# Third group's attention visits two units later, and one key decay issued ahead of a value load

## The chip, the cores and the metric

The kernel runs on one core of one Trainium2 chip. The metric is the device time of one execution in microseconds. Before the change it was 212.03 us, the median of three runs (211.67, 212.03, 212.72).

## The reference

A decayed linear attention over 4 batches, 8 heads, 768 positions and head size 64, followed by a two-layer feed-forward block on the result, all taken by the kernel as float32 and rounded to float16 when loaded:

```python
for b in range(nb):                      # blocks of 64 positions
    intra = (qb @ kb.T) * Dmask          # Dmask[i, j] = lam ** (i - j) for i >= j, else 0
    intra = intra @ vb
    inter = (qb * lam_pow) @ kv_state
    out[block] = intra + inter
    kv_state = lam_block * kv_state + (kb * rev_pow).T @ vb
x = out as [3072 tokens, 512]
h = x @ w_in                             # 512 x 2048
g = h * tanh(softplus(h))                # Mish
result = g @ w_out                       # 2048 x 512
```

## The kernel before

The kernel works in chunks of 128 positions instead of 64. There are six chunk rows (groups n = 0 to 5) of four batches each, so 24 chunks, numbered c = 4n + b. Chunk 8 is the first of the third group, n = 2. All names below carry such a number in words only; in the profile the buffers of one name are not told apart.

For each chunk the loads bring k, q and v from memory (tiles `kn`, `qn`, `vz`; lines L68, L76, L79), all issued by POOL. The key is multiplied by its decay (`ktil`, line L266, function `scale_k`), on POOL for chunks 4 to 19. From the third group on, `turn` (L275) has SP issue two transposing transfers for each chunk, one for q (`qraw`, waits for the load of q) and one for the decayed key (`kraw`, waits for `ktil`).

The attention of a group of four chunks is done in **visits**, two chunks at a time: `pair_s` (L343, L349) multiplies `kraw` by `qraw` into `pS` and adds the state's part to `pO`; DVE masks `pS` into `sb` (L358); `pair_o` (L370) multiplies `sb` by `vz`; DVE scales the outcome into `xtok` (L376); and SP issues two transposing transfers `xt<-xtok` (L380). The four blocks of `xt` of one group are the input of the first feed-forward product of that group. `pair_a` (L319) brings the state forward: DVE adds (`raws`, L323) and POOL multiplies (`wc`, L324).

The feed-forward block is the dense work of PE. `mm1_unit` (L399, four matmuls with 512 columns) makes one of 16 slices of h for the whole group; ACT applies Mish to it (`hsg`, L406). `mm2_unit` (L431, four matmuls with 512 columns) makes a quarter of the output of one chunk; after the fourth quarter ACT copies `po` to `osb` (L446) and issues the store.

The order is written out by hand, and every engine keeps it. There are three stretches:

- **The head.** Groups 0 and 1 are done with PE transposes (`first_t`, L217: `pk` and `pq`), `first_s` (L237) and `first_o` (L252, L256); PE also runs the first group's `mm1_unit`s and then the second group's in pieces (`mm1_tile`, L417). POOL issues the loads of chunks 4 to 7 and the weights `wout` (L107) in a list, and between them the key decays of chunks 4 to 7.
- **The double period** (n = 1 of the last loop). PE runs 32 `mm2_unit`s, u = 0 to 31, for the first two groups. Into them the visits of the third group are set at the numbers in `steps`. POOL issues k and q of chunks 12 to 15 after units 7, 11, 15 and 19, v of chunks 12 and 13 after unit 23, and v of 14 and 15 after unit 27, each time behind a one-element copy (`tick`, L387) from the output tile that ACT has just written. `turn` of chunk 12 stands after unit 21 and that of chunk 13 after unit 23.
- **The single periods** (n = 2 to 5): 16 `mm1_unit`s and 16 `mm2_unit`s of one group, with the visits of the next.

Within one unit number, the visit is written ahead of the loads and of `turn`, since it is entered in `todo` first.

Of the kernel before, what the change touches and what calls it, by code (L numbers as in the profile page):

```python
# [13 lines left out]
def bc(ap, axis, n):  # L14
    shape = list(ap.shape)
    shape.insert(axis, n)
    return ap.unsqueeze(axis).broadcast_to(shape)
# [3 lines left out]
def kernel(  # L21
# [11 lines left out]
    B, H, S, D = q.shape  # L33
# [10 lines left out]
    NT = 2  # L44
# [13 lines left out]
    def chunk_rows(t, i):  # L58
        n, b = divmod(i, B)
        return t[b, :, n * C : (n + 1) * C, :].rearrange("h p c -> p h c")  # L60
# [9 lines left out]
    def load_q(i):  # L70
        if i == 0:
            qn[i] = const.tile([128, H, D], F32, name="qn0")
            nc.scalar.dma_start(out=qn[i], in_=chunk_rows(q, i))
            return
        qn[i] = loads.tile([128, H, D], F16, name="qn", tag="qn")
        nc.gpsimd.dma_start(out=qn[i], in_=chunk_rows(q, i))  # L76

    def load_v(i):
        nc.gpsimd.dma_start(out=vz[i % NVB][:, :, 0:D], in_=chunk_rows(v, i))  # L79
# [25 lines left out]
    def load_wout(s):  # L105
        w = DF // WS
        nc.gpsimd.dma_start(  # L107
            out=wout[s],
            in_=moe_w_out[s * w : (s + 1) * w, :].rearrange("(k p) f -> p k f", p=128),
        )  # L110
# [152 lines left out]
    def scale_k(i):  # L263

        t = work.tile([128, H, D], F16, name="ktil", tag="ktil", bufs=8)
        (nc.vector if i < B or i >= (NG - 1) * B else nc.gpsimd).tensor_tensor(  # L266
            out=t, in0=kn[i], in1=bc(lk, 2, D), op=ALU.mult)
        ktil[i] = t
# [117 lines left out]
    def behind(src):  # L386
        nc.gpsimd.tensor_copy(tick, src)  # L387
# [118 lines left out]
    for i in range(B, NVB - 2):  # L506
# [5 lines left out]
    load_k(NVB - 1)  # L512
    scale_k(B + 1)
    load_q(NVB - 1)
    load_v(NVB - 1)
    scale_k(B + 2)
    load_wout(0)
    load_wout(1)
    scale_k(B + 3)
# [4 lines left out]
    steps = {11: ((first_t, 4),), 13: ((first_s, 4),), 14: ((first_t, 5),),  # L524
             15: ((first_o, 4), (first_s, 5), (first_t, 6))}
# [14 lines left out]
    for f, i in ((load_k, c + 1), (load_q, c + 1), (load_k, c + 2), (load_q, c + 2)):  # L540
        f(i)
    steps = {(4, 0): ((first_o, 5), (first_s, 6)), (4, 1): ((first_t, 7), (state_step, 0)),
             (4, 2): ((first_o, 6), (first_s, 7), (state_step, 1)), (4, 3): ((state_step, 2),),
             (5, 0): ((first_o, 7), (state_step, 3))}
# [10 lines left out]
    for n in range(NT - 1, NG):  # L555
        dense = [(mm2_unit, m, b, part) for m in ((0, 1) if n < NT else (n,))
                 for b in range(B) for part in range(WS)]
        if n >= NT:
            dense = [(mm1_unit, n, ni) for ni in range(NKI)] + dense
        todo = {}  # L560

        def at(u, f, *args):
            todo.setdefault(u, []).append((f, args))

        if n + 1 < NG:
            pairs = []
            for b in (0, 2):
                s = Pair()
                s.n, s.b = n + 1, b
                pairs.append(s)  # L570
            steps = (((9, pair_s, 0), (13, pair_o, 0), (16, pair_s, 1), (20, pair_o, 1),
                      (24, pair_a, 1)) if n < NT else
                     ((4, pair_s, 0), (8, pair_o, 0), (13, pair_s, 1), (17, pair_o, 1),
                      (20, pair_a, 1)))
            for u, f, b in steps:
                at(u, f, pairs[b])
        if n == NT:
            at(0, lambda: behind(hsg[n][0:1, 0, 0:1]))
            at(0, turn, (n + 1) * B + 2)
            at(0, turn, (n + 1) * B + 3)  # L580
        if n + 2 < NG:
            c = (n + 2) * B
            loads_ = [(f, c + b) for b in range(B) for f in (load_k, load_q)]
            loads_ += [(load_v, c + b) for b in range(B)]
            for x, (f, i) in enumerate(loads_):
                if n >= NT:
                    u = (1, 2, 3, 5, 6, 8, 10, 11, 12, 13, 14, 15)[x]
                    at(u, lambda u=u: behind(hsg[n][0:1, u, 0:1]))
                else:
                    u = 7 + x // 2 * 4  # L590
                    if x % 2 == 0:
                        at(u, lambda: behind(last_out[0][0:1, 0:1]))
                at(u, f, i)
            for b, u in enumerate((21, 23) if n < NT else (18, 19, 21, 23)):
                at(u, turn, c + b)
        for u, (fn, *args) in enumerate(dense):
            fn(*args)
            for f2, args in todo.get(u, ()):
                if args and isinstance(args[0], Pair):
                    args[0].spare = "po" if u < NKI - 1 and n >= NT else "ph"  # L600
                f2(*args)
# [30 lines left out]
```

## Time and profile before

| what | value |
| --- | --- |
| time, median of three runs | 212.03 us |
| the profiled execution's own time | 213.28 us |
| its span, first to last instruction | 211.5 us |
| granted TensorE clock, mean | 1.000 |
| PE busy | 203.1 us, 96% of the span |
| POOL, ACT, DVE busy | 102.4, 86.3, 69.3 us |
| double period on PE | 54.9 to 87.4 us |
| transfers moved | 26.76 MB, mean 127 GB/s |

The span leaves 1.78 us of the execution's own time outside. A row of a timeline gives the start and the length in microseconds, then engine, line, operation, what is written and read, the count, and in brackets how long the engine had been idle and what released it. In a list of transfers, the last number is the time from the issue to the landing. A lone `PEld` is the weight load that runs beside PE's matmuls, and an engine's name with a `q` is its sequencer.

### The profile page before, as it was taken

How to read it: one execution, taken by the hardware profiler on the slowest of the kernel's cores; microseconds unless marked ns; L12 is line 12 of the kernel's file. 1: busy time of each engine (PE TensorE's matmuls, PEld its weight loads, DVE VectorE, ACT ScalarE, POOL GpSimd, SP SyncE). 2: the span in 40 equal slices, each digit the busy share in tenths (PEclk: the TensorE clock that was granted, in tenths of full speed). 3: DMA queues.
4: the chain of work that ended last, by engine and by line, in shares of the span. 5: the costliest groups of instructions: out<-in, count | busy, mean ns of one | idle time of the engine just before them, and what ended most of it. 6: DMA issues, size and time to landing. Idle time of an engine off the chain costs nothing.

```text
span 211.5 us, 4241 instructions
## 1 busy us (share of the span) xinstructions
PE 203.1 (96%) x1728; PEld 110.2 (52%) x1728; DVE 69.3 (33%) x131; ACT 86.3 (41%) x146; POOL 102.4 (48%) x149
## 2 busy tenths in 40 slices
PE   7798999999997999999999999999999999999994
PEld 2465546999644544455544454544445544444442
DVE  6867746650004442042440042582042600000000
ACT  5664566656321111356412356312456221566120
POOL 7997379948992558796965076931000000000000
PEclk9999999999999999999999999999999999999999
DMA  9999999999999999999996999996902032100112
GB/s 132 132 159 172 192 145 115 152 195 168 114 146 209 195 179 177 171 188 148 149 161 152 190 81 84 144 167 152 183 1 51 3 99 99 51 3 0 50 50 99
DMA packets 109894, 26.76 MB, mean 127 GB/s; under 512 B 102578, under 2 KB 106930, under 8 KB 109874
## 3 DMA queue, kind: packets, MB, share of 16 engines
q0 software_dynamic: 78080, 13.37, 91.8%
q1 hardware_dynamic: 27296, 6.63, 20.4%
q10 hardware_dynamic: 4498, 6.49, 9.9%
q8 instruction: 13, 0.21, 0.5%
q14 instruction: 7, 0.06, 0.1%
HBM read 27.26 MB, written 6.29 MB: 159 GB/s over the span
## 4 chain that ended last, share of the span: by engine, by line
PE 75%; POOL 13%; DMA 9%; issue 1%; DVE 0%; POOLq 0%
PE po L431 35%; PE ph L399 27%; DMA kn<-in_k_dram 6%; PE ph L417 5%; DMA kraw<-ktil 3%; POOL vz L79 3%; POOL ktil L266 3%; POOL qn L76 2%; POOL kn L68 2%; PE pS L343 2%; PE pO L370 2%; POOL win L92 1%; POOL win L95 1%; PE pv L319 1%; PE pO L349 1%
## 5 line engine op out<-in xcount | busy, mean ns | idle before, releaser
L431 PE MATMUL po<-wout,hsg 128*128 128x512 f16 (+2 forms) x400 | 85.4, 371 | 0.0
L399 PE MATMUL ph<-xt,win 128*128 128x512 f16 (+2 forms) x332 | 73.5, 371 | 0.4 <-ACT hsg L406 0.2
L406 ACT ACTIVATE hsg<-ph 128x512 f16<-128x512 f32 x80 | 47.5, 597 | 30.2 <-PE ph L399 29.8
L431 PEld LDWEIGHTS <-hsg 128*128 128x128 f16 x400 | 37.8, 98 | 42.3
L399 PEld LDWEIGHTS <-win 128*128 128x128 f16 x332 | 30.9, 98 | 34.7 <-issue 1.5
L446 ACT ACTIVATE osb<-po 128x512 f32<-128x512 f32 (+1 forms) x24 | 14.2, 593 | 75.4 <-PE po L431 70.6
L358 DVE TENSOR_TENSOR sb<-pS,maskT 128x512 f16<-128x512 f32 x32 | 20.0, 683 | 64.0 <-PE pS L343 64.0
L68 POOL DMA_DIRECT2D kn<-in_k_dram x23 | 20.9, 909 | 5.3 <-issue 1.9
L79 POOL DMA_DIRECT2D vz<-in_v_dram x24 | 21.6, 905 | 2.7 <-DMA win<-in_moe_w_in_dram 2.0
L76 POOL DMA_DIRECT2D qn<-in_q_dram x23 | 20.8, 903 | 3.3 <-DMA wout<-in_moe_w_out_dram 1.9
L266 POOL TENSOR_TENSOR ktil<-kn,lk 128x512 f16<-128x512 f16 x16 | 16.6, 1050 | 3.0 <-ACT hsg L406 2.9
L376 DVE TENSOR_TENSOR xtok<-pO,lqt 128x512 f16<-128x512 f32 x16 | 10.3, 686 | 16.8 <-PE pO L370 16.8
L417 PE MATMUL ph<-xt,win 128*128 128x128 f16 x256 | 15.3, 219 | 0.0
L417 PEld LDWEIGHTS <-win 128*128 128x128 f16 x256 | 14.5, 98 | 0.1
L440 DVE COPY osb<-po 128x128 f32<-128x128 f32 x1 | 0.3, 290 | 38.7 <-PE po L431 38.7
L421 ACT ACTIVATE hsg<-ph 128x512 f16<-128x512 f32 x16 | 9.6, 597 | 6.9 <-PE ph L417 6.9
L387 POOL COPY tick<-hsg 1x1 f16<-1x1 f16 x25 | 4.4, 176 | 12.2 <-ACT hsg L406 12.1
L324 POOL TENSOR_TENSOR wc<-raws,lbc 128x512 f16<-128x512 f32 x6 | 6.6, 1113 | 5.5 <-DVE raws L323 5.5
L163 PE MATMUL busy<-kzero 128*128 128x512 f16 x18 | 7.6, 516 | 1.2 <-DVE kzero L149 1.2
L266 DVE TENSOR_TENSOR ktil<-kn,lk 128x512 f16<-128x512 f16 (+1 forms) x8 | 6.6, 846 | 0.0
L241 DVE TENSOR_TENSOR sb<-pS,maskT 128x512 f16<-128x512 f32 x8 | 5.2, 686 | 4.2 <-PE pS L237 4.2
L343 PE MATMUL pS<-qraw,kraw 64*128 64x128 f16 x128 | 5.1, 218 | 1.2 <-DMA kraw<-ktil 1.2
(72 smaller groups left out, 122.6 us busy)
## 6 DMA issues: line engine op xcount, KB each, us to landing
out_dram<-osb ACTq DMA_DIRECT2D x23, 256.0 KB, 2.6
vz<-in_v_dram POOLq DMA_DIRECT2D x24, 128.0 KB, 4.7
kn<-in_k_dram POOLq DMA_DIRECT2D x23, 128.0 KB, 5.2
qn<-in_q_dram POOLq DMA_DIRECT2D x23, 128.0 KB, 5.0
wout<-in_moe_w_out_dram POOLq DMA_DIRECT2D x4, 512.0 KB, 10.4
win<-in_moe_w_in_dram POOLq DMA_DIRECT2D x3, 512.0 KB, 10.2
kn<-in_k_dram SPq DMA_DIRECT2D x1, 256.0 KB, 3.2
qn<-in_q_dram ACTq DMA_DIRECT2D x1, 256.0 KB, 3.9
```

Of the source, the lines that this page charges most:

```text
L68: nc.gpsimd.dma_start(out=kn[i], in_=chunk_rows(k, i))
L76: nc.gpsimd.dma_start(out=qn[i], in_=chunk_rows(q, i))
L79: nc.gpsimd.dma_start(out=vz[i % NVB][:, :, 0:D], in_=chunk_rows(v, i))
L266: (nc.vector if i < B or i >= (NG - 1) * B else nc.gpsimd).tensor_tensor(out=t, in0=kn[i], in1=bc(lk, 2, D), op=ALU.mult)
L358: nc.vector.tensor_tensor(out=s.sb[x][t], in0=pS[x][t], in1=bc(maskT, 1, JP), op=ALU.mult)
L376: nc.vector.tensor_tensor(out=xtok[:, :, :, t, :], in0=s.pO[t], in1=bc(bc(lqj[:, :, t], 1, 2), 3, D), op=ALU.mult)
L399: nc.tensor.matmul(ph_t[ni][:, lo:hi], win_t(ni, kc), xt[n][:, kc, lo:hi], start=(kc == 0), stop=(kc == NKC - 1))
L406: nc.scalar.activation(hsg[n][:, ni, :], ph_t.pop(ni), AF.Mish)
L417: nc.tensor.matmul(ph[:, u, :], win_t(w * s + u, kc), xt[n][:, kc, b * C : (b + 1) * C], start=(kc == 0), stop=(kc == NKC - 1),)
L421: nc.scalar.activation(hsg[n][:, w * s : w * s + w, b * C : (b + 1) * C], ph, AF.Mish)
L431: nc.tensor.matmul(po[:, lo:hi], hsg[n][:, ki, b * C : (b + 1) * C], wout[part][:, kk, lo:hi], start=(ki == 0), stop=(ki == NKI - 1),)
L446: nc.scalar.activation(o, i, AF.Copy)
```

## The change

Two edits.

In the head, `scale_k(6)` (here `scale_k(B + 2)`) is put ahead of `load_v(7)` (here `load_v(NVB - 1)`). In the double period the five visits of the third group are set two units later: `pair_s` of chunks 8 and 9 after unit 11 instead of 9, its `pair_o` after 15 instead of 13, `pair_s` of chunks 10 and 11 after 18 instead of 16, its `pair_o` after 22 instead of 20, and `pair_a` after 26 instead of 24. The loads, `turn` and the single periods keep their numbers.

```diff
     load_k(NVB - 1)
     scale_k(B + 1)
     load_q(NVB - 1)
+    scale_k(B + 2)
     load_v(NVB - 1)
-    scale_k(B + 2)
     load_wout(0)
     load_wout(1)
     scale_k(B + 3)
...
-            steps = (((9, pair_s, 0), (13, pair_o, 0), (16, pair_s, 1), (20, pair_o, 1),
-                      (24, pair_a, 1)) if n < NT else
+            steps = (((11, pair_s, 0), (15, pair_o, 0), (18, pair_s, 1), (22, pair_o, 1),
+                      (26, pair_a, 1)) if n < NT else
                      ((4, pair_s, 0), (8, pair_o, 0), (13, pair_s, 1), (17, pair_o, 1),
                       (20, pair_a, 1)))
```

On POOL, in the head, around the load of v of chunk 7 (`vz_76`); the two decays shown are those of chunks 5 and 6, and `wout_83`, `wout_84` are the first two quarters of the second weight:

```order
 L266 TENSOR_TENSOR ktil<-kn,lk 128x512
 L76 DMA qn<-in_q_dram 128x8x64
+L266 TENSOR_TENSOR ktil<-kn,lk 128x512
 L79 DMA vz_76<-in_v_dram 128x8x64
-L266 TENSOR_TENSOR ktil<-kn,lk 128x512
 L107 DMA wout_83<-in_moe_w_out_dram 128x4x512
 L107 DMA wout_84<-in_moe_w_out_dram 128x4x512
```

The decay of chunk 6 moved past the issue of one load; everything behind the pair stands where it stood.

On SP, in the double period: the transfers of chunk 11's `turn`, then `xt` of the third group's four chunks, then the `turn`s of chunks 12 and 13:

```order
 L275 DMA_TRANSPOSE qraw<-qn 128x4x128
 L275 DMA_TRANSPOSE kraw<-ktil 128x4x128
-L380 DMA_TRANSPOSE xt<-xtok 128x4x128 x4
+L380 DMA_TRANSPOSE xt<-xtok 128x4x128 x2
 L275 DMA_TRANSPOSE qraw<-qn 128x4x128
 L275 DMA_TRANSPOSE kraw<-ktil 128x4x128
+L380 DMA_TRANSPOSE xt<-xtok 128x4x128 x2
 L275 DMA_TRANSPOSE qraw<-qn 128x4x128
 L275 DMA_TRANSPOSE kraw<-ktil 128x4x128
```

Since `pair_o` moved from unit 20 past unit 21, chunk 12's `turn` now stands on SP's queue between the first two and the last two transfers of `xt`.

## The prediction

> **What bounds the kernel.** I read the page's busy times first, then its chain of work that ended last, then PE's list of waits.
>
> ```profile
> PE   203.1 (96%) x1728; PEld 110.2 (52%) x1728; DVE 69.3 (33%) x131; ACT 86.3 (41%) x146; POOL 102.4 (48%) x149
> ...
> PE 75%; POOL 13%; DMA 9%; issue 1%; DVE 0%; POOLq 0%
> ```
>
> PE is busy for 96% of the span, and three quarters of the chain are PE's. The rest is POOL and transfers, so the chain leaves PE in a few places only. PE's waits name them:
>
> ```profile
> PE pS L343 <- DMA kraw<-ktil: 1.2, 1, 1.2
> ...
> PE pk L217 <- POOL ktil L266: 0.3, 1, 0.3
> ...
> PE ph L399 <- ACT hsg L406: 0.2, 1, 0.2
> ```
>
> The change aims at the first (once, 1.2 us) and the second (once, 0.3 us). The third matters below. All dense work behind is on PE, so a microsecond taken out of PE's row in the double period comes off the end, unless a later wait takes it back.
>
> **First term: the visit that waited.** PE's timeline at the first `pair_s` of the third group, and then at the second, which did not wait:
>
> ```profile
> 63.64 0.40 PE L343 MATMUL pS<-qraw,kraw 64*128 64x128 f16 x8
> 65.23 0.40 PE L343 MATMUL pS<-qraw,kraw 64*128 64x128 f16 x8 [1.19 <-DMA kraw<-ktil]
> 65.46 0.40 PE L349 MATMUL pO<-wc,qraw 64*128 64x64 f16 x16
> 65.79 0.39 PE L431 MATMUL po<-wout,hsg 128*128 128x512 f16 x1
> ```
>
> ```profile
> 72.41 0.62 PE L343 MATMUL pS<-qraw,kraw 64*128 64x128 f16 x16
> 72.87 0.40 PE L349 MATMUL pO<-wc,qraw 64*128 64x64 f16 x16
> 73.20 3.63 PE L431 MATMUL po<-wout,hsg 128*128 128x512 f16 x16
> 76.66 0.51 PE L370 MATMUL pO<-vz,sb 128*128 128x64 f16 x12
> ```
>
> From start to start the first visit holds PE for 65.79 - 63.64 = 2.15 us and the second for 73.20 - 72.41 = 0.79 us. The wait costs **1.36 us**; the 1.19 in brackets begins only at a modelled end. Sixteen dense matmuls take 76.66 - 73.20 = 3.46 us, so one unit of four is 0.865 us and two units are 1.73 us. What PE waited for:
>
> ```profile
> 58.47 6.72 DMA kraw<-ktil
> ```
>
> This row of the chain is chunk 9's `kraw`: issued at 58.47, landed 6.72 us later, at 65.2. Nothing in the change moves its issue: POOL's and SP's rows ahead of it keep their order. PE, two units later, comes to chunk 8 at 63.64 + 1.73 = 65.37 and to chunk 9 0.23 us later (65.46 - 65.23, eight matmuls), at 65.60. The wait is then gone with 0.37 us to spare; if the head gives PE its 0.33 us (below), the spare is 0.04 us. So I take 1.36 us saved, less 0.1 us for so thin a margin; the ends are 1.36 and 1.0.
>
> Next late could be the second visit, which needs chunk 11's `kraw`:
>
> ```profile
> 64.98 1.37 SPq L275 DMA_TRANSPOSE kraw<-ktil  x1
> ```
>
> ```profile
> kraw<-ktil SPq DMA_TRANSPOSE x1, 6.7
> ```
>
> It landed at 71.7. The visit moves by +1.73 - 1.69 (both savings), to 72.45, and needs it 0.23 us later. Unit 11 ended at 65.79 + 1.73 = 67.5, behind the waiting visit, and now ends ahead of it, at 63.64 + 1.73 - 0.33 = 65.0; so its store and the loads of chunk 13 go out 2.5 us earlier and share the transfer engines with it; 0.98 us covers that, and I cost it at nothing. DVE follows `pair_s` with the same four masks and the same four units before `pair_o`.
>
> **Second term: the head.** POOL's and PE's timelines there:
>
> ```profile
> 33.60 0.89 POOL L79 DMA_DIRECT2D vz<-in_v_dram  x1
> 34.49 1.07 POOL L266 TENSOR_TENSOR ktil<-kn,lk 128x512 f16<-128x512 f16 x1
> 35.48 0.82 POOL L107 DMA_DIRECT2D wout<-in_moe_w_out_dram  x1
> ```
>
> ```profile
> 35.62 0.40 PE L217 MATMUL pk<-ident,ktil 128*128 128x128 f16 x4 [0.33 <-POOL ktil L266]
> ...
> 37.03 0.28 PE L256 MATMUL pO<-sb,vz 128*128 128x128 f16 x2
> ```
>
> The decay now starts at 33.60 and ends by 34.67, if its key has landed. It has:
>
> ```profile
> 24.22 0.87 POOL L68 DMA_DIRECT2D kn<-in_k_dram  x1 [1.66 <-DMA win<-in_moe_w_in_dram]
> ```
>
> ```profile
> kn<-in_k_dram POOLq DMA_DIRECT2D x1, 128.0 KB, 8.7
> ```
>
> 24.22 + 8.7 = 32.9. PE would come at 35.62 - 0.33 = 35.29, so the **0.33 us** go. Next late is DVE's mask of chunk 5, which the L256 row reads, now at 36.70:
>
> ```profile
> 35.33 1.29 DVE L241 TENSOR_TENSOR sb<-pS,maskT 128x512 f16<-128x512 f32 x2 [1.17 <-PE pS L237]
> ```
>
> It ends at 36.62, so the gain stands, barely; its ends are 0 and 0.33. The load of v of chunk 7 goes out 1.07 us later. It is first read by the last `first_o`,
>
> ```profile
> 44.25 0.28 PE L256 MATMUL pO<-sb,vz 128*128 128x128 f16 x2
> ```
>
> about 10 us after its issue, and the `wout` issues behind it stand at the same time. If it pushed `wout` by its own 1 us, POOL's next wait on `wout` would pass that to `ktil` of chunk 9 and so to `kraw`; that is the 0.1 us taken off above, with 0.36 as its end.
>
> **Third term: `xt` behind a `turn`.** The new order on SP puts chunk 12's `kraw` ahead of the last two `xt`, and it waits for POOL:
>
> ```profile
> 79.00 1.06 POOL L266 TENSOR_TENSOR ktil<-kn,lk 128x512 f16<-128x512 f16 x1
> ```
>
> ```profile
> 78.62 2.52 SPq L380 DMA_TRANSPOSE xt<-xtok  x2
> 81.24 1.26 SPq L275 DMA_TRANSPOSE qraw<-qn  x1
> 82.59 1.22 SPq L275 DMA_TRANSPOSE kraw<-ktil  x1
> ```
>
> ```profile
> 87.36 4.01 PE L399 MATMUL ph<-xt,win 128*128 128x512 f16 x17
> ```
>
> The first row is chunk 12's decay; the second holds the `xt` of chunks 10 and 11, the next two are chunk 12's `turn`; the last is the first `mm1_unit` of the first single period. The decay ended at 80.06. It stands on POOL behind the loads that wait for the output of unit 19, ahead of which the same visits stand as before, so it moves by the whole saving, to 80.06 - 1.69 = 78.37. `kraw` of chunk 12 is issued then, and `xt` of chunk 10 one issue later (82.59 - 81.24 = 1.35), at 79.77; its data is ready at 78.62 + 1.73 - 1.69 = 78.66, so SP's queue decides. `xt` of chunk 11 follows half of the 2.52 us later, at 81.0, against 79.86 (below) before. How long does it take to land? Two rows bound it, that transfer's own and that of `kraw` of chunk 12, which had about the same loads around it as `xt` will have:
>
> ```profile
> 79.86 1.28 SPq L380 DMA_TRANSPOSE xt<-xtok  x1
> ```
>
> ```profile
> xt<-xtok SPq DMA_TRANSPOSE x1, 4.9
> ```
>
> ```profile
> kraw<-ktil SPq DMA_TRANSPOSE x1, 5.2
> ```
>
> So it lands at 85.9 to 86.2. PE asks for all four blocks at 87.36 - 1.69 = 85.67. Before it had 87.36 - 84.8 = 2.6 us of slack; now it **waits 0.2 to 0.5 us**, a wait that takes the place of the old one. Against it, PE's 0.2 us on `hsg` just behind may go, because ACT's last `osb` is then further ahead. I take +0.3; the ends are 0 and 0.55. Everything after that (single periods, stores) hangs on PE and shifts along.
>
> One rule speaks for less. The Trainium skill, DMA: Bandwidth & Descriptors, Queues, rings and completion order, says that each transfer engine takes turns between the queues that have work. By that rule SP's `xt` would not stand behind POOL's loads. The trace bears it out only in part: the first `xt` took
>
> ```profile
> xt<-xtok SPq DMA_TRANSPOSE x1, 3.5
> ```
>
> which is the rule's side (its sum would be -1.36 + 0.1 - 0.33 = -1.6, the first rival below), but 4.9 to 6.7 is what the other transposes quoted here took beside loads.
>
> **The sum.** -1.36 + 0.1 - 0.33 + 0.3 = -1.29 us on the profiled execution: 213.28 gives 212.0. But that execution lies 1.25 us above the median of the timed runs, which spread over 1.05 us themselves. A wait on a transfer is just what can differ between executions: if all of the 1.25 were in it, a timed run would gain 0.04 us; if none, 1.29. I keep a quarter of the 1.25 out, 0.3 us, and forecast a gain of 1.0: **211.0 us**. About 0.5% (1.06 us) is what a measurement of this kernel can tell from no change, and the forecast lies at that edge.
>
> **Rivals.**
>
> - *No new wait.* `xt` lands 3.5 us after its issue, at 84.5, ahead of 85.67. Then -1.69: 210.3. For it: the 3.5 row; against it: the two v loads of chunks 12 and 13, which now go out before that `xt`. Chance 0.12.
> - *The wait was the profiled execution's own.* Timed runs met `kraw` nearly in time, or it is later by as much as the visit. Only the head's 0.33 and a little remain: 211.7. The 1.25 us speak for it. Chance 0.15.
> - *`xt` eats the gain.* It lands 1.3 to 1.7 us after PE asks: about 212.0. This takes 6.0 to 6.4 us to land; the `kraw` rows of 6.7 speak for it. Chance 0.12.
> - *Slower.* The same place, worse. The gain is gone when the landing takes 81.0 + x = 85.67 + 1.69, x = 6.4 us, and the kernel is slower by over 0.5% from x = 7.4. The slowest row nearby is a load of q behind other loads:
>
> ```profile
> qn<-in_q_dram POOLq DMA_DIRECT2D x1, 128.0 KB, 8.3
> ```
>
> With 8.3 the wait is 3.6 us and the kernel 214.0. Against it, the slowest transpose of the whole run is one of `qraw`, at 6.9:
>
> ```profile
> DMA to landing us min/median/max: 2.4/4.5/6.9
> ```
>
> Chance 0.08.
>
> The forecast's case, 210.6 to 211.5, keeps 0.53, about half of it (0.26) beyond 0.5%.
>
> **The chances** are then 0.26 + 0.12 = 0.38 for faster by over 0.5%, 0.27 + 0.15 + 0.12 = 0.54 within it, 0.08 slower. The range reaches from the case without a new wait, 210.2, to where the gain is eaten and a little is lost, 212.4.
>
> **What would show it.** The wait on `kraw` and the wait on `ktil` at L217 vanish from PE's list, and the first `pair_s` holds PE 0.79 us. A wait of L399 on `xt<-xtok` appears at the start of the first single period, 0.2 to 0.5 us, with `kraw` of chunk 12 on SP right ahead of the two `xt`. The forecast is wrong if `kraw` of chunk 9 or 11 still holds PE, if `xt` takes over 6 us, or if the runs before never had the wait.

## The result, and the profile after

| | runs | median | lowest to highest |
| --- | --- | --- | --- |
| before | 22 | 211.86 us | 210.84 to 213.25 us |
| after | 22 | 213.04 us | 212.00 to 216.89 us |

The ratio of the mean times is 1.0064, with a 95% interval of 1.0039 to 1.0088: the change makes the kernel slower, by 1.2 us in the median and 1.3 us in the mean. The one run of 216.89 us was in a slower state of the chip, and ratios here leave such runs out. The profiled execution of after took 212.75 us, with a span of 211.0 us. The forecast was 211.0 us with a range of 210.2 to 212.4 us, so it was wrong in size and in sign.

First the page of after, its busy times and its chain:

```profile
PE 202.5 (96%) x1728; PEld 110.2 (52%) x1728; DVE 69.3 (33%) x131; ACT 86.2 (41%) x146; POOL 102.4 (49%) x149
...
PE 86%; DMA 6%; DVE 2%; ACT 2%; issue 1%; SPq 1%; ACTq 0%; POOL 0%; DVEq 0%; POOLq 0%
```

POOL, 13% of the chain before, is out of it. Some 21 us of its part lay in the head, up to L217's wait on `ktil`, and some 5 us led to the late `kraw`; after has neither wait. PE's list of waits in after shows what it has instead:

```profile
PE ph L399 <- DMA xt<-xtok: 1.7, 1, 1.7
PE busy L163 <- DVE kzero L149: 1.2, 1, 1.2
...
PE ph L399 <- ACT hsg L406: 0.2, 1, 0.2
```

Both waits that the change aims at, L343 on `kraw` and L217 on `ktil`, are gone. One new wait stands at the top of the list, and it is longer than the two together. PE's timeline in after, at the first visit and then at the end of the double period:

```profile
64.50 0.62 PE L343 MATMUL pS<-qraw,kraw 64*128 64x128 f16 x16
...
80.79 4.49 PE L431 MATMUL po<-wout,hsg 128*128 128x512 f16 x20
87.00 4.48 PE L399 MATMUL ph<-xt,win 128*128 128x512 f16 x20 [1.72 <-DMA xt<-xtok]
```

The first visit runs through (16 matmuls in one row, no bracket). The last 20 matmuls of the double period start at 80.79; the same 20 take 4.33 us where nothing waits behind them (85.11 - 80.78, in the kernel with later loads, quoted in the seventh experiment), so PE was ready at 85.12 and began at 87.00. **The wait costs 1.88 us.** What led to it, from the chain of after:

```profile
79.13 1.38 SPq L380
80.56 6.20 DMA xt<-xtok
87.00 4.48 PE ph L399 x20
```

The last `xt`, that of chunk 11, was issued at 80.56 and landed 6.20 us later, at 86.76. SP's and POOL's timelines of after show why it left so late and what was in flight:

```profile
74.04 1.19 SPq L275 DMA_TRANSPOSE qraw<-qn  x1
77.84 1.19 SPq L275 DMA_TRANSPOSE kraw<-ktil  x1
79.13 2.75 SPq L380 DMA_TRANSPOSE xt<-xtok  x2
```

```profile
76.76 1.06 POOL L266 TENSOR_TENSOR ktil<-kn,lk 128x512 f16<-128x512 f16 x1
...
78.91 1.83 POOL L79 DMA_DIRECT2D vz<-in_v_dram  x2 [0.28 <-issue]
```

SP stands 2.6 us at chunk 12's `kraw` until POOL ends its decay at 77.82, then issues `kraw`, then both `xt`. Meanwhile POOL issues the two loads of v, at 78.91 and 79.86, so the last `xt` goes out behind both. The second took 6.6 us:

```profile
vz<-in_v_dram POOLq DMA_DIRECT2D x1, 128.0 KB, 6.6
```

The two landed at 84.44 and 86.47, and `xt` 0.3 us after the second.

### The profile page after: what moved, and what is told of

The parts are those of the page before. It is cut to its first block, busy times and chain, and to the rows that moved or that the text cites. A ratio compares the mean times of both kernels' runs of the same rounds, so it can differ in the third digit from the quotient of the medians.

```text
span 211.0 us, 4242 instructions
## 1 busy us (share of the span) xinstructions
PE 202.5 (96%) x1728; PEld 110.2 (52%) x1728; DVE 69.3 (33%) x131; ACT 86.2 (41%) x146; POOL 102.4 (49%) x149
## 4 chain that ended last, share of the span: by engine, by line
PE 86%; DMA 6%; DVE 2%; ACT 2%; issue 1%; SPq 1%; ACTq 0%; POOL 0%; DVEq 0%; POOLq 0%
PE po L431 35%; PE ph L399 32%; PE ph L417 6%; DMA xt<-xtok 3%; PE pS L343 2%; DMA qn<-in_q_dram 2%; PE pO L256 2%; PE pS L237 2%; DMA out_dram<-osb 2%; PE pO L370 2%; PE busy L163 1%; PE pk L217 1%; PE pO L349 1%; ACT osb L446 1%; PE pv L289 1%
## 5 line engine op out<-in xcount | busy, mean ns | idle before, releaser
L399 PE MATMUL ph<-xt,win 128*128 128x512 f16 (+2 forms) x332 | 73.4, 371 | 2.2 <-DMA xt<-xtok 1.7
L399 PEld LDWEIGHTS <-win 128*128 128x128 f16 x332 | 30.9, 98 | 36.5 <-issue 3.4
L258 ACT ACTIVATE xt<-pO 128x512 f16<-128x512 f32 x8 | 4.8, 597 | 3.4 <-PE pO L256 3.1
```

What stands on the lines that cost most here:

```text
L399: nc.tensor.matmul(ph_t[ni][:, lo:hi], win_t(ni, kc), xt[n][:, kc, lo:hi], start=(kc == 0), stop=(kc == NKC - 1))
```

## The experiments

Every ratio is against the kernel before, in runs on the same chip. "Lead" is the time from the issue of chunk 11's `xt` to the moment when PE is ready to read it.

**1. Before, unchanged, profiled again.**

> The kernel before, unchanged, looked at once more. Theory T (the wait of the first pair_s on kraw, 1.36 us in the one profile of before, is rare; the changed kernel loses at the start of the first single period, where xt of chunk 11 lands late behind the turn of chunk 12): no wait on kraw, or under 0.4 us, the kraw of chunk 9 landed before 63.3 us, own time about 212, and mm1 of the third group starts without a wait, xt landed over 1 us earlier. Rival K (the wait on kraw is the usual state): again about 1.2 us in PE's list, own time about 213.

It took 211.51 us, 1.8 less than the profiled execution on which the prediction's sum was made. PE's list of waits begins:

```profile
PE busy L163 <- DVE kzero L149: 1.2, 1, 1.2
PE pq L217 <- DVE q L470: 0.7, 1, 0.7
```

The wait on `kraw` is not there: chunk 9's `kraw` landed at 63.34 instead of 65.2, and PE reads it at 63.48. L217's wait on `ktil` has left the list, but not quite the timeline:

```profile
34.69 0.40 PE L237 MATMUL pS<-pqT,pkT 64*128 64x128 f16 x8
35.23 0.40 PE L217 MATMUL pk<-ident,ktil 128*128 128x128 f16 x4
```

L217 starts 0.54 us behind L237 here, and 0.33 us behind it in after (34.42 and 34.75), where nothing holds it. POOL's decay ended at 35.18, so L217 still lost 0.2 us to it, of 0.39 us by the same count in the first profiled execution.

**2. Before against itself, timed.**

> The kernel before against itself, to size what the comparison can tell, with a third look at it. Theory T: ratio 0.998 to 1.002; no wait on kraw above 0.4 us and none on xt, xt issued 7.4 to 7.6 us ahead of the first mm1 of the third group and landed 2.0 to 2.6 us ahead of it. Rival K (the wait on kraw is common): a wait of 0.5 us or more.

211.80 us, ratio 1.0004 [0.9985, 1.0023]. Over all comparisons, 6 of 162 timed runs of before were longer than the 213.28 us of the profiled one. This profiled execution (211.50 us), too, has no wait on `kraw`, and it serves as the usual run below. Its PE, SP and POOL timelines at the end of the double period:

```profile
85.58 4.66 PE L399 MATMUL ph<-xt,win 128*128 128x512 f16 x20
```

```profile
76.84 2.53 SPq L380 DMA_TRANSPOSE xt<-xtok  x2
79.47 1.30 SPq L275 DMA_TRANSPOSE qraw<-qn  x1
```

```profile
79.37 1.83 POOL L79 DMA_DIRECT2D vz<-in_v_dram  x2 [0.27 <-issue]
```

Here both `xt` go out ahead of the loads of v; the last, at 78.08, landed 5.37 us later, at 83.45, which is 2.1 us before PE asks. After starts L399 at 87.00, 1.42 us later. That is the wait of 1.88 less 0.46, since the double period began at 54.04 in after and at 54.50 here; 0.18 us comes back in the first 20 matmuls behind the wait (91.41 - 87.00 = 4.41 against 90.17 - 85.58 = 4.59). The sum, 1.24 us, is the difference of the two executions, 212.75 - 211.50 = 1.25.

**3. The head's edit alone, and the visits' alone.** `scale_k(B + 2)` ahead of `load_v(NVB - 1)` with the old steps (twice), and the new steps with the old head.

```diff
+    scale_k(B + 2)
     load_v(NVB - 1)
-    scale_k(B + 2)
```

> Only the decay of chunk 6 ahead of the load of v of chunk 7; visits as before. Theory T: no loss, the wait of L217 on ktil gone where there was one, ratio 0.997 to 1.001, no wait on xt. Rival H (the later load of v pushes wout and the loads behind it, and this is the loss): ratio 1.004 to 1.008, and a larger wait on kraw than before.

> Only the decay of chunk 6 ahead of the load of v of chunk 7, once more, since the first comparison (1.0022, 0.9997 to 1.0047) left open if it costs. Theory T (the usual run of before has no wait of L217 on ktil, so the edit moves nothing on PE): ratio 0.999 to 1.001. Rival H (it costs some 0.4 us, a third of the loss, by later loads): ratio 1.001 to 1.004 again.

> Only the visits two units later; the head as before. Theory T: all of the loss, ratio 1.004 to 1.010, a wait of L399 on xt of 1.0 to 2.0 us, chunk 12's kraw issued right ahead of the last two xt. Rival H: ratio 0.995 to 1.001.

The head alone: 1.0022 [0.9997, 1.0047] and 1.0013 [0.9988, 1.0038]. Both intervals hold no change and neither shows a gain; both middle values lie above 1.001, outside what was expected, so a cost of a tenth or two of a per cent is not ruled out. On PE the edit does what it was meant to do. In eight profiled executions with the old head, L217 lost 0.39 us twice, 0.21 and 0.13 once each, and nothing in four; in ten with the edit it lost nothing. That is 0.14 us on average, too little for these timings. Nor does it show at the double period's start, at 54.51 us on average in the ten (54.03 to 55.15) and 54.46 in the eight (54.11 to 54.91); so the 0.46 above is not the edit's. The visits alone: 1.0041 [1.0014, 1.0068], with this wait:

```profile
PE ph L399 <- DMA xt<-xtok: 1.1, 1, 1.1
```

The slowdown is the visits' part, and the new wait comes with it.

**4. Chunk 12's `turn` behind the two `xt`** (after, with `turn` one unit later).

```diff
-            for b, u in enumerate((21, 23) if n < NT else (18, 19, 21, 23)):
+            for b, u in enumerate((22, 23) if n < NT else (18, 19, 21, 23)):
```

> The changed kernel with chunk 12's turn after unit 22 in place of 21, so that it stands behind the last two xt on SP, as before. Theory T: these xt go out about 1 us earlier against PE and meet one transfer less, so the wait of L399 on xt falls from 1.7 to 0 to 0.6 us, and the ratio to before is 0.996 to 1.003. Rival S (two units later leave too little time whatever stands on SP, because of the loads in flight): the wait stays at 1.2 us or more, xt takes 6 us or more to land, ratio 1.004 or more.

1.0109 [1.0069, 1.0149]: worse, which was not expected. PE's timeline shows the old place better and a new one:

```profile
86.46 4.48 PE L399 MATMUL ph<-xt,win 128*128 128x512 f16 x20 [0.69 <-DMA xt<-xtok]
90.86 0.40 PE L343 MATMUL pS<-qraw,kraw 64*128 64x128 f16 x8
93.27 0.40 PE L343 MATMUL pS<-qraw,kraw 64*128 64x128 f16 x8 [2.00 <-DMA kraw<-ktil]
```

The lead grew from 4.56 to 5.77 us and the wait fell to 0.85, but `kraw` of chunk 13, pushed back to 85.53 on SP, now held the next visit. Putting one transfer ahead of another here made one wait shorter and brought another. In the fifth experiment the same transfer went out at 84.99 and held nobody, so its landing, up to 7.7 us here, was long besides. The two waits are about the 2.9 us by which this profiled execution (214.37 us) lies above the usual run; how often the timed runs have both, one execution can't say.

**5. Chunk 12's q ahead, its key behind the `xt`.** After, with the two transfers of that `turn` apart (`half_turn` issues one of them): q's at unit 21, the key's behind both `xt`, and chunk 12's decay ahead of either.

```diff
+            if n < NT:
+                at(21, scale_k, c)
+                at(21, half_turn, c, qn, "qraw", qraw)
+                at(22, half_turn, c, ktil, "kraw", kraw)
+                at(23, turn, c + 1)
-            for b, u in enumerate((21, 23) if n < NT else (18, 19, 21, 23)):
+            for b, u in enumerate(() if n < NT else (18, 19, 21, 23)):
```

> The changed kernel with only chunk 12's kraw moved behind the last two xt on SP; its qraw, which waits for nothing by then, stays ahead of them, and chunk 13's turn keeps its place. Theory T (kraw of chunk 12, waiting for its decay on POOL, is what holds xt): xt goes out about 1 us earlier against PE than in the changed kernel, the wait of L399 on xt is 0.2 to 0.8 us (1.7 there), the new wait on kraw of the run with the whole turn behind (2.0 us, chunk 13's) is under 0.4 us, ratio 1.000 to 1.004. Rival S (the loads in flight alone make xt late): the wait on xt stays at 1.2 us or more, ratio 1.004 or more.

1.0033 [1.0003, 1.0064], by its middle half of the loss; the profiled execution also lost 1.0 us at the second visit, to chunk 11's `kraw`. The lead is 5.77 again and the landing takes 6.30 us, so the wait stays at 0.78 (four added lines make L399 L403 here):

```profile
87.28 4.48 PE L403 MATMUL ph<-xt,win 128*128 128x512 f16 x20 [0.61 <-DMA xt<-xtok]
```

5.77 is the 7.50 of before less two units (1.73). After's 4.56 is 1.2 less again: the first `xt` goes out 1.0 us later against PE, since `kraw` with its wait for the decay is ahead of it, and the second follows 0.2 us later behind the first. What the lead leaves of the wait is the landing.

**6. The loads of v of chunks 12 and 13 two units later** (number 25 instead of 23), on after and on the fifth.

```diff
-                    u = 7 + x // 2 * 4
+                    u = 7 + x // 2 * 4 + 2 * (x in (8, 9))
```

> The changed kernel with the loads of v of chunks 12 and 13 after unit 25 instead of 23, so that they go out behind the last xt instead of just ahead. chunk 12's kraw stays ahead of the xt on SP. Theory L (the loads in flight add about 1 us to the landing of xt): xt of chunk 11 takes 4.6 to 5.3 us instead of 6.2, the lead stays 4.5 us, the wait on xt falls to 0.2 to 0.9 us, ratio 1.001 to 1.004. Rival Q (only SP's own queue counts): xt still takes 5.6 us or more, ratio 1.004 or more.

> The changed kernel with chunk 12's kraw behind the last xt (as in the run with its qraw first) and the two v loads after unit 25. If lead and landing time together are the whole loss: lead 5.8 us, landing 4.6 to 5.4 us, no wait on xt, ratio 0.998 to 1.002. If something else of the change costs (the head, or later visits as such): no wait on xt, and still 1.002 or more.

1.005 [1.0026, 1.0073] and 1.0016 [0.9986, 1.0047]. The first did not do what it was meant to: the load waits for the output written last, and at unit 25 that is still the one of unit 23, so POOL issued it all the same at

```profile
79.44 1.83 POOL L79 DMA_DIRECT2D vz<-in_v_dram  x2
```

and `xt` was late by 1.11 us. It is no test of the loads.

**7. The same loads behind the next output** (number 27), on after, on the fifth, on after again, and on before.

```diff
-                    u = 7 + x // 2 * 4
+                    u = min(7 + x // 2 * 4 + 4 * (x in (8, 9)), 27)
```

> The changed kernel with the loads of v of chunks 12 and 13 behind the output of unit 27, some 4 us later, so that they really go out behind the last xt (moving them to unit 25 had them still wait for unit 23's output and go out at the same time). SP's order as in the changed kernel. Theory L (those loads add about 1 us to the landing of xt): they are issued after 83 us, xt of chunk 11 takes 3.5 to 5.0 us, the lead stays 4.5 us, the wait on xt is 0 to 0.7 us, ratio 1.000 to 1.003. Rival Q (only what stands on SP's queue counts): xt takes 5.5 us or more, the wait is 1.0 us or more, ratio 1.004 or more.

> The same, with chunk 12's kraw behind the last xt. If lead (5.8 us) and landing time (3.5 to 5.0 us) are the whole loss of the changed kernel: no wait on xt, ratio 0.998 to 1.001, below the 1.0016 of the run with the loads at unit 25. If later visits or the head cost something else: no wait on xt, and 1.002 or more.

> The changed kernel with the v loads of chunks 12 and 13 behind the output of unit 27, once more, since its first comparison (0.9975, 0.9948 to 1.0002) left open if it beats before. Theory L: no wait on xt, xt lands in 3.3 to 4.5 us, ratio 0.996 to 1.000. If the first was luck: ratio 1.000 to 1.003.

> The kernel before with only those v loads behind the output of unit 27: head and visits as before. If the later visits bring something of their own once xt is in time: ratio 0.999 to 1.001 here, above that of the changed kernel with the same loads. If the loads alone made that ratio: 0.996 to 0.999 here too.

On after, the SP, POOL and PE timelines and the transfer list at the issue of the last `xt` (its last number is the time to landing):

```profile
77.83 1.19 SPq L275 DMA_TRANSPOSE kraw<-ktil  x1
79.12 2.58 SPq L380 DMA_TRANSPOSE xt<-xtok  x2
```

```profile
83.58 1.83 POOL L79 DMA_DIRECT2D vz<-in_v_dram  x2
```

```profile
80.78 4.49 PE L431 MATMUL po<-wout,hsg 128*128 128x512 f16 x20
85.11 4.67 PE L399 MATMUL ph<-xt,win 128*128 128x512 f16 x20
```

```profile
xt<-xtok SPq DMA_TRANSPOSE x1, 3.3
```

SP issues `kraw` and the two `xt` when it did in after, to 0.12 us. The loads have moved, to 83.58 and 84.53, and `xt` lands 3.3 us after its issue instead of 6.2; PE has no wait. The repeat, and the kernel of the fifth experiment with the loads moved, show the same:

| kernel | lead, us | landing, us | wait of L399 on `xt`, us | ratio, 95% interval |
| --- | --- | --- | --- | --- |
| before (second experiment) | 7.50 | 5.37 | none | 1.0004 [0.9985, 1.0023] |
| after | 4.56 | 6.20 | 1.88 | 1.0064 [1.0039, 1.0088] |
| visits alone | 4.57 | 5.57 | 1.27 | 1.0041 [1.0014, 1.0068] |
| `turn` behind `xt` | 5.77 | 6.37 | 0.85, and 2.0 on `kraw` | 1.0109 [1.0069, 1.0149] |
| after, loads at 25 | 4.43 | 5.30 | 1.11 | 1.0050 [1.0026, 1.0073] |
| q ahead, key behind | 5.77 | 6.30 | 0.78 | 1.0033 [1.0003, 1.0064] |
| q ahead, key behind, loads at 25 | 5.77 | 5.93 | 0.44 | 1.0016 [0.9986, 1.0047] |
| after, loads at 27 | 4.67 | 3.29 | none | 0.9975 [0.9948, 1.0002] |
| after, loads at 27, repeated | 4.57 | 2.49 | none | 1.0028 [1.0006, 1.0050] |
| q ahead, key behind, loads at 27 | 5.77 | 3.33 | none | 1.0000 [0.9974, 1.0025] |
| before, loads at 27 | 7.50 | 5.29 | none | 1.0003 [0.9981, 1.0025] |

In each row the wait is the landing less the lead, plus 0.2 to 0.3 us from the landing to the first matmul where it was positive. The two timings of "after, loads at 27" lie on both sides of 1 and their intervals don't meet, so the gain of the first is not confirmed. Their profiled executions (211.08 and 212.18 us) differ by what the double period's start differs by (54.03 and 55.15 us); the repeat has a wait of 1.3 us on a weight in the head, which no edit here touches. Why the timed runs differ stays open. The three ratios without the new wait average 1.0001: with the wait taken away the changed kernel is as fast as before, and no faster.

The profiled executions say it more closely, if the head is left out. From the double period's start to the end of an execution's own time, before takes 157.0 us where it has no wait (211.51 - 54.52, 211.50 - 54.50), and so do the three kernels without the new wait (211.08 - 54.03, 212.18 - 55.15, 211.59 - 54.56). After takes 158.7 us (212.75 - 54.04) and the visits alone 158.1 (212.23 - 54.11): 1.7 and 1.1 more, which is each one's wait less the 0.18.

On before the move of the loads does not change the landing of the last `xt`: it is out ahead of them in any case, and lands 5.3 us after its issue at 77.97 with the loads of k and q of chunk 15, issued at 75.34 and 76.22, just ahead of it. But chunk 12's `kraw`, which stands right behind the loads of v in before, gains as `xt` does:

```profile
kraw<-ktil SPq DMA_TRANSPOSE x1, 3.2
```

It took 5.5 and 5.6 us in the first and second experiments. It need not be v: with the visits two units earlier (below) the last `xt` goes out between the loads of k and q of chunk 15, issued at 78.42 and 79.29, some 4 us ahead of the next load of v, and took 6.7 us.

**8. Other places for the visits.** Only the first visit later (11 and 14), all visits one unit later, all two units earlier than before.

```diff
-            steps = (((9, pair_s, 0), (13, pair_o, 0), (16, pair_s, 1), (20, pair_o, 1),
+            steps = (((11, pair_s, 0), (14, pair_o, 0), (16, pair_s, 1), (20, pair_o, 1),
```

> The kernel before with the first pair_s after unit 11 instead of 9 and its pair_o after 14 instead of 13; the second pair and the state keep their units 16, 20 and 24. Theory T: no wait on kraw of chunk 9 and none on xt, since the second pair keeps its place; the usual run of before had no wait there either, so ratio 0.996 to 1.001. Rival M (pair_o only three units behind its pair_s meets DVE's masks, 2.5 us): a wait of L370 on sb or of the second pair_s of 0.2 to 0.6 us, ratio 1.001 to 1.003.

> The kernel before with all visits one unit later (10, 14, 17, 21, 25); the last two xt stay ahead of chunk 12's turn. Theory T: xt had about 2.1 us of slack in the second look at before and loses 0.87 of it, so no wait on xt; chunk 13's kraw goes out 0.9 us later, wait on it 0 to 0.6 us; ratio 0.998 to 1.002. Rival S (later visits as such cost): a wait on xt of 0.5 us or more, ratio 1.002 to 1.005.

> The kernel before with all visits two units earlier (7, 11, 14, 18, 22). Theory T: chunk 9's kraw lands when PE comes for it after unit 9, within some tenths, so that PE, 1.73 us earlier, waits 1.4 to 1.8 us for it, and the time is 0.6 to 1.5 us longer, ratio 1.003 to 1.008. Rival K0 (kraw is there long before, and the wait in the first profile of before was a rare accident): no wait, ratio 0.997 to 1.002.

1.0027 [0.9994, 1.0060], 1.0013 [0.9987, 1.0039] and 1.0023 [0.9989, 1.0057]: none is told from no change, and the third was expected to be slower than that. In the first, the second visit waited although the first did not, which was not expected; in the third, PE came too early for chunk 9's `kraw`. The two waits:

```profile
72.31 0.40 PE L343 MATMUL pS<-qraw,kraw 64*128 64x128 f16 x8 [1.43 <-DMA kraw<-ktil]
```

```profile
63.82 0.40 PE L343 MATMUL pS<-qraw,kraw 64*128 64x128 f16 x8 [1.95 <-DMA kraw<-ktil]
```

With the visits two units earlier the runs spread from 211.07 to 215.31 us. With them one unit later the profiled execution waits neither for `kraw` at these two visits nor for `xt`, without a gain in time.

## Why the prediction was wrong, step by step

- **First term (-1.36 + 0.1): right in mechanism, wrong in size.** The visit's wait was in the profiled execution, and in none of the nine with the visits two units later does the first visit wait. But of six profiled executions with the visits at their old places, four had no wait on `kraw`, one lost 1.36 us, and one (the head's edit alone) 0.14 us at the first visit and 0.77 at the second. In the usual run the term is near 0. The forecast kept a quarter of the 1.25 us between that execution and the median out; all of it should have been. The rival "the wait was the profiled execution's own", given 0.15, described the run that one should have summed for.
- **Chunk 11's `kraw` as next late: right in eight of nine.** It was costed at nothing, and in the nine executions with the visits two units later it held PE once, for 1.0 us (the fifth experiment).
- **Second term (-0.33): right in mechanism, too large.** Ten of ten executions with the edit have no wait on `ktil` at L217, but with the old head it is 0 to 0.39 us, 0.14 on average, and the timings show no gain in two comparisons. Whether the later loads cost as much again stays open.
- **Third term (+0.3): the failing step, in the size of the landing.** That `kraw` of chunk 12 would stand ahead of the `xt` on SP and cut the lead was right to a tenth: 85.67 - 81.0 = 4.67 us by the prediction (its 79.77 should be 78.37 + 1.35 = 79.72, which changes nothing), 4.56 measured. The landing, taken at 4.9 to 5.2 us, was 6.20. The first of the two rows it was taken from is of a transfer ahead of the loads of v. The second, chunk 12's `kraw`, does stand right behind them, as `xt` now does, and took 5.2 us in that execution; but in the six others that kept SP's order and these loads it took 5.31 to 6.45. So the row was of the right kind and at the quick end of a spread which one execution didn't show. The `xt` itself took 5.3 to 6.4 with these loads in flight (after and five variants of it) and 2.5 to 3.3 with them moved away (three variants). The prediction also began PE at the landing, where 0.25 us lie between. The wait came out at 1.88 us instead of 0.2 to 0.5. Even a landing of 5.37 us, the usual run's, would have left 1.06 (5.37 + 0.25 - 4.56), so more of the wait is the shorter lead than the longer landing. With the first two terms at nothing and this one at its +0.3, the time would have been about 212.2 us instead of 213.0.
- **The "slower" rival named the right place with the wrong bar.** It asked for a landing of over 7.4 us, because it first had to use up a gain of 1.69 that the usual run doesn't have. From a usual run, any landing over 4.3 us loses.
- **"No new wait"** rested on a landing of 3.5 us. Beside it the prediction set the turns that each transfer engine takes between queues (the Trainium skill, DMA: Bandwidth & Descriptors, Queues, rings and completion order). In after the landing took 6.20, right behind the second load. Whether the turns are taken, no run here shows; what failed is to read a landing time from them.

That the loads beside it make this landing long is shown by the seventh experiment, where SP issued `kraw` and both `xt` at the same times. That the new wait is the loss is shown by its removal, which brings the ratio back to 1 as far as the timings can tell and the time behind the head back to 157.0 us, and by the sum in the second experiment.

## What to carry to other kernels

Before a wait is priced, look at whether it is in a usual run: a profiled execution 1.2 us above the median of the timed runs may owe just that to the wait in question. When a step is moved later, work out for each transfer that it issues how much lead its reader is left with, and which other transfers it now falls behind, on its own queue and on others. A transfer's landing time depends on the loads in flight with it, and with the same loads it still varied by over 1 us between executions here. Take it from rows with the neighbours that it will have, from several executions, and sum for the slowest as well as for the quickest.

## What the runs showed of the hardware that was not expected

The landing times of the same transfers differ widely between executions. Chunk 9's `kraw` landed at 65.2 us in the profiled execution of before and at 63.3 and 63.4 in the two others. Around this time there is a gap in which almost nothing is moved. Stretches of the profiled execution of before (the last column is GB/s), one row of the list of transfers from 57.8 to 58.4, and SP's issues there:

```profile
57.00:59.00 2.00, 2.00 (x11) 0.88 (x9) 0.00 (x0) 0.44 (x1) 1.98 (x3) 1.00 2.52 152
59.00:60.20 1.20, 1.20 (x7) 0.59 (x6) 0.00 (x0) 0.16 (x1) 1.18 (x2) 1.00 5.39 21
60.20:62.00 1.80, 1.80 (x10) 0.78 (x8) 0.00 (x0) 0.00 (x0) 1.80 (x3) 1.00 1.39 128
```

```profile
q8 instruction: 1, 0.02, 16.2%
```

```profile
57.15 1.27 SPq L275 DMA_TRANSPOSE qraw<-qn  x1
58.47 2.40 SPq L275 DMA_TRANSPOSE kraw<-ktil  x1
```

For 1.2 us the transfer engines move 21 GB/s instead of 128 to 152, and the issue of chunk 9's `kraw` takes 2.40 us instead of 1.27. A fetch of instructions of 16 KB begins at 58.24, ahead of the gap. In the second experiment the fetch begins at 56.73, the gap follows 0.75 us later, and the slow issue is that of the `qraw` ahead (2.36 us). In each of the eighteen profiled executions a stretch under 35 GB/s (averaged over 0.4 us) begins 0.5 to 1.9 us after the start of the fetch that falls between 55 and 59 us, and that of the profiled execution of before is the latest of these fetches. A few such stretches elsewhere have no fetch ahead of them. That the fetch makes the gap, and that its place in time decides which transfer is late, fits these rows but was not tried.
